# Linear attention feeding two MLP stages: constant matmuls at the start, key and query projections issued together, the first half's routing moved to later groups

## The chip, the cores and the metric

One Trainium2 chip, one core of it. The metric is device time in microseconds (us) of one launch, the median of several runs. A profiled execution of the same kernel gives the rows; its times count from the start of its span. The engines are named as the profile names them: PE (TensorE matmul), PEld (its weight loads), DVE (VectorE), ACT (ScalarE), POOL (GpSimd) and SP (SyncE, which issues most DMAs).

## The reference, cut to what matters

```python
# q, k, v: (4, 8, 576, 64); w_phi: (64, 128)
def phi(x):
    proj = einsum('bhsd,df->bhsf', x, w_phi)
    proj = proj - max(abs(proj), axis=-1, keepdims=True)
    return concatenate([exp(proj), exp(-proj)], axis=-1)
q_p, k_p = phi(q), phi(k)
kv = einsum('bhsf,bhsd->bhfd', k_p, v); z = sum(k_p, axis=2)
x = einsum('bhsf,bhfd->bhsd', q_p, kv) / (einsum('bhsf,bhf->bhs', q_p, z) + 1e-6)
# x as 2304 rows of 512: each row goes to the expert (of 8) with the largest
# cosine similarity: x = gate * (relu(x @ w1[e]) @ w2[e])
# then a dense MLP: h = x @ w_in; out = max(0.01 * h, h) @ w_out
```

## The kernel before, in words

Three stages follow each other on the core: attention with routing folded into it (to about 240 us), the expert MLP, and the dense MLP. Every engine runs its instructions in the order in which the program issues them; nothing reorders them. So the order of the Python statements is the order of each queue.

**Attention** (`attention`, line 63) works in 8 units of a batch pair and a head pair, 9 chunks of 128 rows each: 72 chunks, two to a group, so 36 groups and a loop of 38 steps (line 312). Step t issues in this order:

- `proj(t, "k")` (line 145): six PE matmuls of 256 columns into one of three banks `pj`, then on DVE an absolute maximum (L158) and a subtraction (L160) of 128x512.
- `k_exp` of the group before on ACT (L165, L166), loads of the next unit, and `split_in`, which splits raw keys and queries into a high part (ACT, L101) and a low part (POOL; DVE for the very first).
- `kv_fin_c` (line 215) for a unit whose keys are all in: small PE matmuls (L220) and two DVE copies into `kvz` (L224).
- `kv_mm` of group t-2 (L184, 16 PE matmuls). After a unit's last chunk `kv_fin_a` copies its sums on ACT (L201, L203); when that chunk is the first of its group, the group's other half (`rest`) comes later in the step, since it writes the same banks.
- `proj(t, "q")`: the same six matmuls and two DVE instructions for the queries.
- `q_T` of group t-1: four PE transposes into the only bank `dt` (L190), two exponentials on ACT (L193, L194).
- `flush` (squares on ACT, stores of attention rows by SP), the `rest`, `kv_fin_b` (L211 and an ACT copy `kvt`, L213).
- `num(t-8)` (line 227): 16 PE matmuls that read `kvz` (L243), and on DVE a reciprocal and a scaling (L257 to L262). The first `num` of a unit comes in the same step as that unit's `kv_fin_c`. `num`, `kv_fin_b`, `kv_fin_c` and the fillers share two banks `nm`.
- `filler(t)` (line 1406): work of the later stages. With e = t - 26, e from 0 to 9, it holds the routing of the first 1152 rows: one-hot and counts (e = 0, 1), `choose` and `early_rows` (e = 2), `early_rows2`, `early_place` (e = 3), `is_first`, `first_place` (e = 4), three thirds of `marks_v` (L666; e = 3, 4, 5), `early_ids` with nine small PE matmuls that read all marks (L581) and two gathers by POOL (e = 5), four weight loads (e = 6), `e_x`, which transposes the gathered rows and splits them on ACT and DVE (L931, L952, L953; e = 7), and `moe.split` of weight chunks 0 to 3 (ACT L906, DVE L907; two at e = 8, two at e = 9, with loads of chunks 4 to 7).

After step 37 the last six `num` run (lines 371 to 376), each after a call of `tail`, which splits weight chunks 4 and 5 on the way. `setup_en1` to `setup_en3` prepare the expert embeddings in steps 2 to 4.

Of the kernel before, what the change touches and what calls it, by code (L numbers as in the profile page):

```python
# [8 lines left out]
F32 = mybir.dt.float32  # L9
# [16 lines left out]
F64_MIN = 2.0  # L26
F64_MAX = 2.0 ** 16 * (122880.0 - 2.0 ** -7)
LAG = 8
SPL = {3: (0, "k"), 4: (0, "q"), 6: (1, "k"), 7: (1, "q")}
KL = 2  # L30
QL = 1
# [31 lines left out]
def attention(ctx, late_ctx, tc, consts, in_p, kqT, vx, w_phi, emb, tau, xd, lg, nsq, filler, tail, stores):  # L63
    nc = tc.nc
# [6 lines left out]
    ps_nm, kv_ctx = psum("ps_nm", 2), late_ctx.enter_context(ExitStack())  # L71
# [9 lines left out]
    def load(u, js=(0, 1)):  # L81
        bp, hp = units[u]
        d = st[u]
        for j in js:
            s, e = CUT[j]
            d["raw", j] = in_p.tile([128, 2, 640], F32, tag="raw", name="raw")
            for i in (slice(0, 1), slice(1, 2)) if u == 0 else (slice(0, 2),):
                nc.sync.dma_start(out=d["raw", j][:, i, 0:e - s], in_=kqT[bp, hp, :, i, s:e])
# [6 lines left out]
    def split_in(u, j, nms=("k", "q"), eng=None):  # L95
        d = st[u]
        for nm in nms:
            n = CUT[j][1] - CUT[j][0]
            d[nm, j] = in_p.tile([128, 2, 640], F32R, tag=nm, name=nm)
            raw, hi, lo = d["raw", j][:, "kq".index(nm), 0:n], d[nm, j][:, 0, 0:n], d[nm, j][:, 1, 0:n]  # L100
            nc.scalar.activation(hi, raw, AF.Copy)  # L101
            (eng or nc.gpsimd).tensor_tensor(lo, raw, hi.bitcast(F32), ALU.subtract)

    def setup():
        wb = cp.tile([128, 256], F32, name="wb")
        nc.scalar.dma_start(out=wb, in_=w_phi)
        whi = cp.tile([128, 256], F32R, name="whi")
        wlo = cp.tile([128, 256], F32R, name="wlo")
        nc.vector.tensor_copy(whi, wb)
        nc.vector.tensor_tensor(wlo, wb, whi.bitcast(F32), ALU.subtract)  # L110
        consts["w"] = (whi, wlo)
        nc.vector.memset(cp.tile([128, 16], F32, name="cpad"), 0.0)
# [32 lines left out]
    def proj(t, nm):  # L145
        whi, wlo = consts["w"]
        p = ps_pj.tile([128, 512], F32, tag="pj", name="pj")
        for i, (u, c) in enumerate(groups[t]):
            j = int(c >= 4)
            hi, lo = st[u][nm, j][:, 0], st[u][nm, j][:, 1]  # L150
            s = slice((c - 4 * j) * 128, (c - 4 * j) * 128 + 128)
            o = p[:, i * 256:(i + 1) * 256]
            nc.tensor.matmul(o, hi[:, s], whi, start=True, stop=False)
            nc.tensor.matmul(o, hi[:, s], wlo, start=False, stop=False)
            nc.tensor.matmul(o, lo[:, s], whi, start=False, stop=True)
        pv = p.rearrange("p (g f) -> p g f", f=128)
        m = sm.tile([128, 4, 1], F32, tag="m" + nm, name="m")
        nc.vector.tensor_reduce(m[:, :, 0], pv, X, ALU.max, apply_absolute_value=True)  # L158
        dd = wk.tile([128, 4, 128], F32, tag="d" + nm, name="dd")
        nc.vector.tensor_tensor(dd, pv, m.to_broadcast([128, 4, 128]), ALU.subtract)  # L160
        return dd

    def k_exp(dd):
        kp = wk.tile([128, 2, 4, 128], F32, tag="kp", name="kp")
        nc.scalar.activation(kp[:, 0], dd, AF.Exp)  # L165
        nc.scalar.activation(kp[:, 1], dd, AF.Exp, scale=-1.0)  # L166
        return kp
# [127 lines left out]
    wk = Pools(tc, ctx, "a_wk", {"dk": 3, "dq": 2, "kp": KL + 1})  # L295
    ps_pj, ps_dt = [ctx.enter_context(tc.tile_pool(name=n, bufs=b, space=PSUM, side="right")) for n, b in (("ps_pj", 3), ("ps_dt", 1))]
    load(0)
    setup()
    split_in(0, 0, eng=nc.vector)
    load_v(0)  # L300
# [11 lines left out]
    for t in range(T + 2):  # L312
        more = t < T
        if more:
            dk = proj(t, "k")
        if t - 1 in dks:
            kps[t - 1] = k_exp(dks.pop(t - 1))
        if more:
            dks[t] = dk
            for u, c in groups[t]:  # L320
                if c == 0 and u < U - 1:
                    load(u + 1, (0,) if u == 0 else (0, 1))
                if c == 2 and u == 0:
                    load(1, (1,))
                if c == 6 and 0 < u < U - 1:
                    load_v(u + 1)
                if c in SPL and u + 1 < U:
                    split_in(u + 1, *SPL[c])
        while post:
            kv_fin_c(post.pop())  # L330
        due = [i for i in sorted(kps) if i <= t - KL or not more]
        rest, last = [], fin
        fin = []
        for i in due:
            kp = kps.pop(i)
            g = groups[i]
            kv_mm(i, 0, kp)
            if g[0][1] == 8:
                kv_fin_a(g[0][0])
                fin.append(g[0][0])  # L340
                rest.append((i, kp))
            else:
                kv_mm(i, 1, kp)
                if g[1][1] == 8:
                    kv_fin_a(g[1][0])
                    fin.append(g[1][0])
        if more:
            dq = proj(t, "q")
        for i in sorted(dqs):
            if i <= t - QL and t < T or t > T or i < T - 1 and t == T:  # L350
                qps[i] = q_T(dqs.pop(i))
        if more:
            dqs[t] = dq
        flush()
        for i, kp in rest:
            kv_mm(i, 1, kp)
        if not more:
            last, fin = last + fin, []
        for u0 in last:
            kv_fin_b(u0)  # L360
            post.append(u0)
        if ready() and (done <= t - LAG or not more):
            num(done, qps.pop(done))
            done += 1
        if t in (2, 3, 4):
            (setup_en1, setup_en2, setup_en3)[t - 2](*et)
        if more:
            filler(t, ps)
# [1016 lines left out]
def body(ctx, tc, kqT, vx, w_phi, emb, tau, wm, wd, out):  # L1385
    nc = tc.nc
# [6 lines left out]
    consts = {"ident": ident}  # L1393
    xd = dram.tile([NT, DM], F32, name="xd")
    yt = dram.tile([4, 128, YW], F32, name="yt")
    with tc.manual_schedule(), ExitStack() as r_ctx:
        ff = Ffn(tc, yt, wd, out)
        ro = ff.ro = Router(r_ctx, tc, lambda: ff.open_w(r_ctx))
        lg, nsq = ro.lg, ro.nsq
        with ExitStack() as m_ctx:  # L1400
            moe = Moe(tc, consts, ro, xd, yt, wm)
            moe.open_raw(m_ctx)
# [3 lines left out]
            def filler(n, ps):  # L1406
                if n == CONVERT - 4:
                    ff.fetch(0)
                elif 0 <= n - CONVERT < 7:
                    ff.convert(0, n - CONVERT)  # L1410
                e = n - (18 + LAG)
                if e == 0:
                    ro.onehot(0, 9)
                elif e == 1:
                    ro.rk = ps()[:, 0:10 * NE].rearrange("p (b e) -> p b e", e=NE)
                    ro.count(0, 9)
                    ro.ranks()
                elif e == 2:
                    ro.choose()
                    ro.early_rows()  # L1420
                elif e == 3:
                    ro.early_rows2()
                    ro.early_place()
                elif e == 4:
                    ro.is_first(0, 9)
                    ro.first_place(0, 9)
                if 3 <= e <= 5:
                    ro.marks_v(3 * e - 9, 3 * e - 6)
                if e == 5:
                    ro.early_ids(ps())  # L1430
                    for i in range(NEARLY):
                        moe.gather(i)
                elif e == 6:
                    for c in range(4):
                        moe.load(0, c)
                elif e == 7:
                    moe.e_open()
                    for i in range(NEARLY):
                        moe.e_x(i, ps())
                elif e in (8, 9):  # L1440
                    for c in (2 * e - 16, 2 * e - 15):
                        moe.split(0, c, more=False)
                    for c in (4, 5) if e == 9 else ():
                        moe.load(0, c)
                    for c in (6, 7) if e == 9 else ():
                        moe.load(0, c)

            left = []
# [1 line left out]
            def tail(i):  # L1450

                if not left:
                    left.append(0)
                    ro.ps, ro.ps_k = [r_ctx.enter_context(tc.tile_pool(name=n, bufs=1, space=PSUM, side="right", reuse_waits="tile"))
                                      for n in ("ps_r", "ps_k")]
                    moe.open(m_ctx)
                    ro.rk = ro.ps_k.tile([128, 19, NE], F32, tag="rk", name="rk")
                elif i in (-5, -3):
                    moe.split(0, 4 + (i + 5) // 2, more=False)

# [48 lines left out]
            more = []  # L1509
# [92 lines left out]
```

## Time and profile before

| | before |
|---|---|
| median of 3 runs (lowest, highest) | 910.33 us (909.57, 913.11) |
| the profiled execution's own time | 910.88 us |
| its span in the profile | 909.2 us |
| busy PE / DVE / ACT / POOL | 879.3 / 537.9 / 414.7 / 154.1 us |

The span lies 1.7 us below the time of its own execution. Busy shares are means over stages with different limits, so what counts is which engine ended the waits of PE in the stage that the change touches. The granted clock is the share of TensorE's full speed that was granted in a stretch. A row of the time line gives start, duration, engine, line, the tile written and the tiles read; brackets give the idle time before it and what ended that.

### The profile page before, as it was taken

To read this page: it belongs to the slowest core of one execution; us is meant where nothing else is said; L and a number is where in the kernel's file an instruction comes from. 1 tells how busy PE (TensorE), PEld (TensorE's weight loads), DVE (VectorE), ACT (ScalarE), POOL (GpSimd) and SP (SyncE) were. 2 spreads that over 40 slices of the span, in tenths; PEclk is the share of its full clock that TensorE was granted. 3 is DMA by queue.
4 is the path that set the end of the run, shared out by engine and by line. 5 is a ranking of instruction groups with operands and counts; after the bars stand their busy time and mean duration, and the time that the engine had idled before them with its cause. 6 is when DMAs were issued, how large, how long until landed. Compare 5 with 4: busy or idle time off the path is not lost. (4 is left out here: it accounts for less than half of the span.)

```text
span 909.2 us, 16064 instructions
## 1 busy us (share of the span) xinstructions
PE 879.3 (97%) x6388; PEld 830.8 (91%) x6388; DVE 537.9 (59%) x980; ACT 414.7 (46%) x782; POOL 154.1 (17%) x188
## 2 busy tenths in 40 slices
PE   7999999899999999999999999999999999999996
PEld 6999999899999999999988899999999999999995
DVE  6677666856866236556654576666666666643332
ACT  6777665546335233445555553334333344532221
POOL 4344232211110100101000021111121111101112
PEclk9999999989999999999999999999999999999998
DMA  5442332133166224575742612111111211001111
GB/s 193 158 129 77 106 102 80 49 133 124 52 243 221 79 70 138 193 228 181 231 143 87 194 50 91 47 47 47 48 60 48 79 47 47 1 12 48 47 47 58
DMA packets 40755, 91.66 MB, mean 101 GB/s; under 512 B 3720, under 2 KB 22792, under 8 KB 38624
## 3 DMA queue, kind: packets, MB, share of 16 engines
q1 hardware_dynamic: 37360, 80.13, 26.9%
q0 software_dynamic: 3168, 10.29, 3.4%
q8 instruction: 52, 0.85, 0.4%
q14 instruction: 31, 0.25, 0.1%
q10 hardware_dynamic: 144, 0.13, 0.1%
HBM read 75.53 MB, written 15.01 MB: 100 GB/s over the span
## 5 line engine op out<-in xcount | busy, mean ns | idle before, releaser
L1299 PE MATMUL pl<-xhi,wihi 128*128 128x256 f32 x560 | 157.4, 281 | 1.4 <-PEq L1162 1.4
L1299 PE MATMUL pl<-xlo,wihi 128*128 128x256 f32 x560 | 157.3, 281 | 0.0
L1299 PE MATMUL pl<-xhi,wilo 128*128 128x256 f32 x560 | 157.2, 281 | 0.0
L1304 ACT ACTIVATE t<-pl 128x512 f32<-128x512 f32 x70 | 41.8, 597 | 192.4 <-PE pl L1299 192.4
L1325 PE MATMUL po<-wohi,ghi 128*128 128x512 f32 x288 | 113.8, 395 | 1.3 <-ACT acc L1330 1.3
L1325 PE MATMUL po<-wohi,glo 128*128 128x512 f32 x288 | 114.1, 396 | 0.0
L1325 PE MATMUL po<-wolo,ghi 128*128 128x512 f32 x288 | 113.9, 396 | 0.0
L1113 PE MATMUL py<-hphi,w 128*128 128x256 f32 (+3 forms) x512 | 108.7, 299 | 1.8 <-DVE w L907 1.8
L1299 PEld LDWEIGHTS pl<-xhi,wihi 128*128 128x128 f32 x560 | 106.0, 189 | 4.3 <-issue 1.6
L1305 DVE TENSOR_TENSOR t<-t,pl 128x512 f32<-128x512 f32 x70 | 48.1, 687 | 103.1 <-ACT t L1304 103.1
L1299 PEld LDWEIGHTS pl<-xlo,wihi 128*128 128x128 f32 x560 | 105.4, 188 | 2.8 <-DVE xlo L1283 0.2
L1299 PEld LDWEIGHTS pl<-xhi,wilo 128*128 128x128 f32 x560 | 105.5, 188 | 0.0
L1096 PE MATMUL pp<-phi,w 128*128 128x256 f32 (+3 forms) x512 | 103.7, 296 | 1.5 <-DVE hplo L1099 1.0
L1247 POOL TENSOR_TENSOR af<-af,wraw 128x512 int32<-128x512 int32 x32 | 47.7, 1510 | 310.1 <-DVE af L1245 310.0
L907 DVE TENSOR_TENSOR w<-raw,w 128x1024 fp32r<-128x1024 f32 x64 | 76.9, 1223 | 16.2 <-ACT w L906 16.2
L1113 PEld LDWEIGHTS py<-hphi,w 128*128 128x128 f32 x512 | 83.8, 188 | 2.6 <-DVE w L907 2.4
L1096 PEld LDWEIGHTS pp<-phi,w 128*128 128x128 f32 x512 | 82.9, 189 | 1.9 <-DVE hplo L1099 1.3
L1096 PE MATMUL pp<-plo,w 128*128 128x256 f32 (+3 forms) x256 | 75.8, 296 | 0.0
L1113 PE MATMUL py<-hplo,w 128*128 128x256 f32 (+3 forms) x256 | 75.6, 295 | 0.0
L184 PE MATMUL kv<-v,kp 128*128 128x65 f32 (+1 forms) x576 | 72.4, 279 | 3.2 <-ACT kp L165 1.5
L184 PEld LDWEIGHTS kv<-v,kp 128*128 128x128 f32 x576 | 69.9, 197 | 4.3 <-ACT kp L165 2.0
L243 PE MATMUL nm<-kvz,qp 128*128 128x73 f32 (+1 forms) x576 | 71.2, 279 | 2.2 <-DVE kvz L224 1.6
(320 smaller groups left out, 1718.9 us busy)
## 6 DMA issues: line engine op xcount, KB each, us to landing
raw<-in_wm_dram SPq DMA_DIRECT2D x64, 512.0 KB, 4.5
wraw<-in_wd_dram SPq DMA_DIRECT2D x16, 1024.0 KB, 4.9
v<-in_v_dram SPq DMA_DIRECT2D x8, 650.0 KB, 4.3
raw<-in_kq_dram SPq DMA_DIRECT2D x7, 640.0 KB, 4.7
xd<-xs SPq DMA_DIRECT2D x32, 128.0 KB, 1.8
raw<-in_kq_dram SPq DMA_DIRECT2D x7, 512.0 KB, 4.2
y<-yt SPq DMA_DIRECT2D x6, 512.0 KB, 4.6
yt<-y SPq DMA_DIRECT2D x16, 128.0 KB, 5.0
```

Of the source, the lines that this page charges most:

```text
L184: nc.tensor.matmul(o, kp[:, f, 2 * i + h, :], r, start=(c == 0 and f == 0), stop=(c == 8 and f == 1), skip_group_check=True)
L243: nc.tensor.matmul(ov, qp[:, f, 2 * i + h, :], r, start=(f == 0), stop=(f == 1))
L907: (eng or nc.vector).tensor_tensor(lo, raw, hi.bitcast(F32), ALU.subtract)
L1096: nc.tensor.matmul(pv[:, m], a[:, c], x[:, k], start=(k == 0 and i == 0), stop=(k == 3 and i == 2))
L1113: nc.tensor.matmul(p, a[:, c], b[:, k], start=(k == 0 and n == 0), stop=(k == 7 and n == 2))
L1247: nc.gpsimd.tensor_tensor(f[:, h], f[:, h], d["li"][:, h], ALU.add)
L1299: nc.tensor.matmul(pv[:, m], a[:, c], x[:, k], start=(k == 0 and n == 0), stop=(k == 3 and n == 2))
L1304: nc.scalar.activation(t, p, AF.Copy, scale=0.01)
L1305: nc.vector.tensor_tensor(t, t, p, ALU.max)
L1325: nc.tensor.matmul(p, a[:, cc], x[:, w], start=(b == bs[0] and k == 0 and n == 0), stop=(b == bs[-1] and k == 1 and n == 2))
```

## The change

It issues 30 matmuls of a constant 128x128 bf16 tile of ones ahead of everything else on PE; their result is not read. It issues the query projection of a step right behind the key projection, so ahead of `k_exp`, `kv_fin_c` and `kv_mm`. It moves routing in `filler`: `early_place` from e = 3 to 4, the thirds of `marks_v` from 3, 4, 5 to 4, 5, 6, `is_first` and `first_place` from 4 to 8, `early_ids` and the gathers from 5 to 7, `e_open` and `e_x` from 7 to 9; chunk 0 is split at e = 8, chunks 1 and 2 at e = 9, chunk 3 in the first call of `tail`.

```diff
+WARM = 30
...
+    def warm():
+        p = ps_nm.tile([128, 512], F32, tag="nm", name="nw")
+        for i in range(WARM):
+            nc.tensor.matmul(p[:, 0:128], consts["ones"], consts["ones"], start=True, stop=True)
...
     load(0)
+    warm()
     setup()
...
         if more:
-            dk = proj(t, "k")
+            dk, dq = proj(t, "k"), proj(t, "q")
...
-        if more:
-            dq = proj(t, "q")
         for i in sorted(dqs):
...
+        consts["ones"] = ro.ones
...
                     ro.early_rows2()
+                elif e == 4:
                     ro.early_place()
-                elif e == 4:
+                elif e == 8:
                     ro.is_first(0, 9)
                     ro.first_place(0, 9)
-                if 3 <= e <= 5:
-                    ro.marks_v(3 * e - 9, 3 * e - 6)
-                if e == 5:
+                if 4 <= e <= 6:
+                    ro.marks_v(3 * e - 12, 3 * e - 9)
+                if e == 7:
                     ro.early_ids(ps())
                     for i in range(NEARLY):
                         moe.gather(i)
                 elif e == 6:
                     for c in range(4):
                         moe.load(0, c)
-                elif e == 7:
+                elif e == 8:
+                    moe.split(0, 0, more=False)
+                elif e == 9:
                     moe.e_open()
                     for i in range(NEARLY):
                         moe.e_x(i, ps())
-                elif e in (8, 9):
-                    for c in (2 * e - 16, 2 * e - 15):
+                    for c in (1, 2):
                         moe.split(0, c, more=False)
-                    for c in (4, 5) if e == 9 else ():
-                        moe.load(0, c)
-                    for c in (6, 7) if e == 9 else ():
+                    for c in range(4, 8):
                         moe.load(0, c)
...
                     ro.rk = ro.ps_k.tile([128, 19, NE], F32, tag="rk", name="rk")
+                    moe.split(0, 3, more=False)
                 elif i in (-5, -3):
```

## Rows read from the trace of the kernel before

**Rows 1.** The page: busy time, and the granted clock in 40 slices.
```profile
PE 879.3 (97%) x6388; PEld 830.8 (91%) x6388; DVE 537.9 (59%) x980; ACT 414.7 (46%) x782; POOL 154.1 (17%) x188
...
PEclk9999999989999999999999999999999999999998
```

**Rows 2.** Windows: busy us of each engine, granted clock, DMA share, GB/s.
```profile
172.00:176.00 4.00, 3.87 (x23) 3.87 (x24) 3.70 (x12) 3.24 (x9) 3.59 (x5) 0.67 0.11 33
176.00:180.00 4.00, 4.00 (x34) 4.00 (x34) 3.38 (x7) 1.39 (x5) 0.00 (x0) 0.91 0.02 4
180.00:184.00 4.00, 2.65 (x29) 2.56 (x29) 2.62 (x8) 1.42 (x4) 1.80 (x3) 0.95 0.24 46
184.00:188.00 4.00, 4.00 (x21) 4.00 (x20) 1.56 (x3) 0.39 (x1) 0.95 (x1) 0.50 0.96 346
188.00:192.00 4.00, 4.00 (x26) 4.00 (x26) 1.11 (x7) 2.42 (x8) 0.00 (x0) 0.70 0.74 296
```

**Rows 3.** Time line of PE around two waits: step 30, and the matmuls of `early_ids`.
```profile
172.13 1.11 PE L243 MATMUL nm<-kvz,qp 128*128 128x73 f32 x8 [1.18 <-DVE kvz L224]
...
181.76 0.23 PE L581 MATMUL ex<-qe,r 128*128 128x6 bf16 x3 [1.35 <-DVE r L666]
```

**Rows 4.** Time line of PE in the start, first `num` included.
```profile
4.66 0.58 PE L153 MATMUL pj<-whi,k 128*128 128x256 f32 x1 [4.66 <-ACT k L101]
...
9.57 0.28 PE L153 MATMUL pj<-whi,q 128*128 128x256 f32 x1
...
20.30 2.30 PE L184 MATMUL kv<-v,kp 128*128 128x130 f32 x16 [1.54 <-ACT kp L165]
...
41.97 1.90 PE L243 MATMUL nm<-kvz,qp 128*128 128x73 f32 x16
...
47.42 1.90 PE L243 MATMUL nm<-kvz,qp 128*128 128x73 f32 x16
```

**Rows 5.** Time line of ACT in the start.
```profile
12.08 0.63 ACT L101 ACTIVATE k<-raw 128x512 fp32r<-128x512 f32 x1 [2.81 <-DMA raw<-in_kq_dram]
...
20.15 0.61 ACT L166 ACTIVATE kp<-dd 128x512 f32<-128x512 f32 x1
```

**Rows 6.** Waits of PE from 0 to 145 us: total, times, longest.
```profile
PE kv L184 <- ACT kvz L203: 1.4, 2, 0.8
PE ke L220 <- ACT kvt L213: 0.5, 1, 0.5
```

**Rows 7.** Time line of PE, a query projection of step 28.
```profile
156.41 0.36 PE L153 MATMUL pj<-whi,q 128*128 128x256 f32 x1
156.61 0.28 PE L154 MATMUL pj<-wlo,q 128*128 128x256 f32 x1
156.73 0.28 PE L155 MATMUL pj<-whi,q 128*128 128x256 f32 x1
```

**Rows 8.** Time line of DVE, end of step 29 to step 31.
```profile
169.73 0.17 DVE L572 TENSOR_TENSOR qe<-iota,s 128x18 bf16<-128x18 f32 x1
...
170.50 0.68 DVE L158 TENSOR_REDUCE m<-pj 128x4 f32<-128x512 f32 x1
...
171.90 0.28 DVE L224 COPY kvz<-ke 128x32 f32<-128x32 f32 x2
...
174.25 0.88 DVE L547 TENSOR_TENSOR sc<-oh,oe 128x72 f32<-128x72 bf16 x1
...
176.20 0.55 DVE L666 TENSOR_TENSOR r<-io,rwf 128x384 bf16<-128x384 f32 x1
```

**Rows 9.** Time line of DVE, PE, ACT and PE, steps 34 to the last `num`.
```profile
204.94 2.38 DVE L907 TENSOR_TENSOR w<-raw,w 128x1024 fp32r<-128x1024 f32 x2 [0.16 <-ACT w L906]
...
208.80 2.01 PE L243 MATMUL nm<-kvz,qp 128*128 128x73 f32 x16 [0.41 <-DVE kvz L224]
...
212.03 0.61 ACT L165 ACTIVATE kp<-dd 128x512 f32<-128x512 f32 x1
...
230.99 1.98 PE L243 MATMUL nm<-kvz,qp 128*128 128x73 f32 x16 [0.47 <-DVE xs L262]
```

## The prediction

> **What bounds the kernel now.** The page comes first: PE is busy for 97% of the span, and its granted clock is at nine tenths or more in every slice but two, the last and the ninth, about 182 to 205 us [rows 1]. So a gain has to come from PE's waits or from its clock, and the ninth slice lies where the first half is routed. Windows of 4 us, laid around that slice, show the clock at 0.67, 0.91, 0.95, 0.50 and 0.70 [rows 2]. PE's time line shows what came before each fall: a wait of 1.18 us in step 30 for the `kvz` copy on DVE, and one of 1.35 us for the marks that `early_ids` reads [rows 3]. [...] In the start, PE idles until 4.66 us and again 1.54 us at 20.30 us, for the key exponentials on ACT [rows 4], and less for `kvz` and `kvt` [rows 6]. From the first `num` at 41.97 us a step lasts 5.45 us (the next `num` starts at 47.42) [rows 4], and up to step 29 PE waits once, for `kvz`, 0.6 us (the 1.4 us less the 0.8 of the start) [rows 6]. The later stages are bound by PE, so what attention gains or loses reaches the end whole.
>
> **The change part by part.** Times go against the profiled execution's own 910.88 us, 0.55 us above the median of 910.33.
>
> **Constant matmuls: nothing.** From 4.66 to 9.57 us PE issues 21 matmuls, 0.23 us each; later they follow each other in 0.12 us [rows 4, 7]. A full clock from the first one on would save up to 21 x 0.11 = 2.3 us there. But PE then stands at 20.30 us until ACT has the key exponentials, and ACT's queue runs without a gap from 12.08 us, when a DMA lets it go on, to the second of these at 20.15 us [rows 4, 5]. None of that depends on how early PE was; what PE wins, it waits longer. With that cover gone the value would be the 2.3 us. Thirty matmuls of 128 columns need no more than half the 0.23 us of 256 columns each, about 3.4 us (an estimate), less than the 4.66 us for which PE is idle; were they twice as long, the delay would fall into the same wait. The row says 0. [...]
>
> **Order of the projections, start: -1.2 us.** In step 4 the query projection, 6 x 0.12 = 0.7 us, now lies in front of the wait that ends at 20.30 us and fills it. In step 8 it lies in front of L220, whose 0.5 us wait for `kvt` it covers [rows 6]. Bounds: 0, if `dt`, the single bank for the transposes, holds PE instead, and 2.0 us, if the first wait for `kvz` (0.8 us) goes too. I take 0.7 + 0.5, since both waits are certain to be preceded by work now.
>
> **Order, steps 9 to 29: -1.7 us.** The first matmul of a projection keeps the second waiting for 0.20 us, others 0.12 [rows 7]. Two projections back to back have one such start fewer per step: 21 steps x 0.08 us. Bounds: 0, if the start of `q_T` behind `kv_mm` costs as much, and 1.7 us. Inside a group no such pause shows when a second chunk follows, so I take 1.7.
>
> **Routing, removed: -1.35 and -5.1 us.** All marks are made by e = 6 and `early_ids` comes at the end of e = 7, a full step later, so its wait goes. If no other wait takes its place, the clock's 5.1 us go as well. The gathers, two steps later, still have two steps until `e_x`; POOL's additions behind them are read only after attention. SP's loads of chunks 4 to 7 keep their place but wait for a later split, and the stores of attention rows queue behind them; the four `xs` buffers cover that.
>
> **Routing and order, step 30: +0.6 us.** DVE is behind in step 30: it runs gapless into the `kvz` copy at 171.90 us. What is taken from in front of it is 169.73 to 170.50 us, 0.77 us. What the new order puts there is the query pair, as long as the key pair, 170.50 to 171.90, 1.40 us [rows 8]. The wait of 1.18 us becomes 1.8.
>
> **Step 35: +1.7 us.** The same copy for the next unit kept PE for 0.41 us behind two weight splits, 2.38 us on DVE [rows 9]. Now one split of 1.19 stands there and `is_first` with `first_place`, 174.25 to 176.20 us, 1.95 [rows 8]: 0.76 us more, and the query pair, 1.40. Bounds +1.4 (the extra falls into time in which the splits wait for ACT anyway) and +2.2. The wait becomes 1.8 to 2.6 us.
>
> **Steps 35 and 36: +0.9 us.** The key exponentials of group 35, at 212.03 us behind two splits [rows 9], now also stand behind two evacuations of `e_x` of 0.6 us, which wait for transposes that follow the delayed `num`. Bounds 0.3 and 1.5 us; I take the middle. `e_x` itself only moves.
>
> **Tail: +1.2 us.** The split of chunk 3, half of 2.38 us, enters DVE's queue ahead of the last six `num`, where PE already waits for DVE's `xs` [rows 9]. Bounds 0.7 (0.47 us of slack) and 1.2.
>
> **Sum.** -1.2 - 1.7 - 1.35 - 5.1 + 0.6 + 1.7 + 0.9 + 1.2 = -4.95: 905.9 us if the clock never falls. But the walk leaves waits of about 1.8 us in step 30, over 2 in step 35, over 1 in step 36. In the attention stage three waits exceeded 1 us: 1.54 (clock stayed full), 1.18 and 1.35 (it fell). I take one fall at the price of the shorter stretch, 1.7 us: **907.6 us**.
>
> **Rivals.**
> - The clock holds: 905.9 us. For it: after 1.54 us at 20.30 the clock stayed full. Against: shorter waits brought it down twice. [...]
> - The start pays: ACT's chain moves with PE after all, 907.6 - 2.3 = 905.3 us. Against: the DMA at 12.08 us.
> - DVE isn't late: nothing is left of the waits in steps 30, 35 and 36, so from 905.9 go 1.8, 2.1 and 0.9: 901.1 us. For: DVE is busy 59% over all. Against: step 30 already waits for DVE with less in front.
> - Two falls: 905.9 + 2 x 1.7 = 909.3 us.
> - Slower, through the new order on DVE: the `kvz` copy stands behind the query pair, PE waits in steps 30, 35 and 36, and after each the clock stays low for the longer stretch, 3.4 us: 905.9 + 10.2 = 916.1 us. It decides from three such falls on; with two it is 912.7.
>
> **How the numbers follow.** Chances: forecast 0.34, clock holds 0.16, start pays 0.05, DVE not late 0.14, two falls 0.23, three long falls 0.08. A measurement of this kernel tells about 0.5% (4.6 us) from no change; against 910.33 that is below 905.8 or above 914.9. Faster: DVE not late 0.14, half of the clock holding 0.08, most of the start 0.04, and a part of the forecast, whose terms with bounds sum to about 3 us to either side, 0.05: 0.31. Slower: three long falls, 0.07. Within: 0.62. The range leaves out most of the last rival and the lower half of "DVE isn't late", and holds two long falls nearly: 902.5 to 912.0 us.
>
> **What would show it.** Right: the first `kv_mm` wait of the start still ends near 20.3 us, and is longer before the query projection fills it; the first `num` at 40 to 41.5 us; steps of 5.37 us up to step 29; no wait at L581; a wait of 1.5 us or more for `kvz` in step 30 and around 2 in step 35, with the granted clock below 1 behind at least one. Wrong: the first `num` before 40 us (the start pays), no `kvz` wait above 1 us (DVE is not late), or a full clock through 160 to 240 us.

## The result, and the profile after

The changed kernel takes 922.52 us (median of 15 executions, 919.95 to 924.14); the kernel before took 910.38 us on the same chips (median of 15, 907.03 to 921.02). The ratio is 1.012, with a 95% interval of 1.0095 to 1.0145: slower by 1.2%, where 907.6 had been forecast. Ratios and intervals, here and below, leave out executions in a slower state, while the times are medians of all, so a ratio differs a little from the quotient of two medians. Single executions of the kernel before spread over 14 us, and those beside the experiments have mean granted clocks from 0.979 (923 us) to 0.998 (906 us): some of them have a clock fall that others lack, so a profile of it is one draw among several.

The profiled execution of the changed kernel has a span of 922.3 us, 13.1 more than before. The page, against [rows 1]:

```profile
PE 890.1 (97%) x6418; PEld 840.5 (91%) x6418; DVE 538.3 (58%) x980; ACT 414.7 (45%) x782; POOL 152.9 (17%) x188
...
PEclk9999999895999999999999899999999999999998
```

PE does 30 matmuls more and is busy 10.8 us longer. Of these, 3.4 us are the constant matmuls, in time in which PE stood idle before, so some 7 of the 13.1 us are slower work and the rest is longer waits. The clock shows where the work is slower: an eight stands in the eighth slice, about 161 to 184 us, a five in the tenth, about 207 to 230 us, and an eight near 510 us. Windows of 6 us of the same kernel (time, PE, PEld, DVE, ACT and POOL busy, clock, DMA share, GB/s):

```profile
168.00:174.00 6.00, 2.32 (x20) 2.18 (x18) 5.28 (x11) 1.77 (x6) 2.12 (x2) 0.88 0.04 13
174.00:180.00 6.00, 6.00 (x33) 6.00 (x32) 4.13 (x10) 1.35 (x3) 0.96 (x3) 0.55 0.08 25
204.00:210.00 6.00, 4.17 (x24) 3.56 (x23) 2.70 (x8) 2.02 (x7) 0.09 (x1) 0.72 0.26 87
210.00:216.00 6.00, 6.00 (x29) 5.98 (x29) 3.75 (x4) 3.88 (x6) 0.34 (x2) 0.50 0.19 53
216.00:222.00 6.00, 5.48 (x27) 5.29 (x26) 0.00 (x0) 2.16 (x9) 0.00 (x0) 0.50 0.64 234
222.00:228.00 6.00, 6.00 (x32) 6.00 (x32) 1.09 (x5) 2.55 (x7) 0.44 (x2) 0.57 0.07 22
...
510.00:516.00 6.00, 3.46 (x16) 3.46 (x17) 1.38 (x3) 0.63 (x1) 0.00 (x0) 0.54 0.46 144
```

What a window loses is put at (1 - clock) x 6 us, an estimate from these clocks. Behind the last of these falls PE's pace goes with it: from 514 to 516 us, at a clock of 0.50, its matmuls of 256 columns start 0.21 us apart, and 0.12 us apart from 500.2 to 502.8 us of the kernel before, at 1.00. By that estimate 3.4 us are lost from 168 to 180, 10.3 us from 204 to 228, where the kernel before had a clock of 1.00 (one of its windows below), and 2.8 us from 510 to 516. The same for the 4 us windows of [rows 2] gives 1.7 us for the first two and 3.4 for the other three: the 5.1 us that the kernel before lost from 172 to 192 are replaced by the 3.4 from 168 to 180.

```profile
210.00:216.00 6.00, 5.28 (x44) 4.87 (x43) 3.25 (x6) 4.49 (x13) 2.21 (x2) 1.00 0.69 240
```

PE's time line in the changed kernel shows what stands ahead of each stretch, and the start:

```profile
1.26 3.38 PE L108 MATMUL nw<-ones 128*128 128x128 bf16 x30 [1.26 <-DVE ones L473]
4.83 0.58 PE L159 MATMUL pj<-whi,k 128*128 128x256 f32 x1 [0.19 <-ACT k L102]
...
20.27 2.30 PE L190 MATMUL kv<-v,kp 128*128 128x130 f32 x16 [0.87 <-ACT kp L171]
...
41.03 1.90 PE L249 MATMUL nm<-kvz,qp 128*128 128x73 f32 x16
...
173.41 1.99 PE L249 MATMUL nm<-kvz,qp 128*128 128x73 f32 x8 [3.68 <-DVE kvz L230]
...
205.89 2.98 PE L249 MATMUL nm<-kvz,qp 128*128 128x73 f32 x16 [1.62 <-DVE kvz L230]
...
508.76 0.35 PE L1304 MATMUL pl<-xhi,wihi 128*128 128x256 f32 x1 [1.47 <-PEq L1167]
512.54 0.58 PE L1304 MATMUL pl<-xlo,wihi 128*128 128x256 f32 x1 [3.42 <-DVE f_pad L1200]
```

The first `pl` matmul of the kernel before:

```profile
499.99 0.35 PE L1299 MATMUL pl<-xhi,wihi 128*128 128x256 f32 x1 [1.40 <-PEq L1162]
```

- **Start.** The constant matmuls end before the first projection, which comes 0.17 us later than before. They do make the projections faster (0.12 us apart from 5.78 us on, where the kernel before, 0.21 us apart from 5.77, gets there at 9.57; the granted clock reads 1.00 in every window from 4 to 10 us of both), but `kv`'s wait takes that back: it still ends at 20.27 us (20.30 in [rows 4]). The first `num` is at 41.03, 0.94 us earlier.
- **Step 30.** The `kvz` wait is 3.68 us, against 1.18 in [rows 3]. The wait of `early_ids` is gone.
- **Step 35.** The `kvz` wait is 1.62 us, against 0.41 in [rows 9]. Behind it the clock is low for some 20 us.
- **Dense stage.** Behind the branch (L1167) a wait of 1.47 us comes ahead of the first `pl` matmul, as before (1.40). A second one, of 3.42 us, stands between the first and the second `pl` matmul; the kernel before has none there. `pl` starts 8.8 us later than before (499.99 there), so 4.3 of the 13.1 us are lost behind that point.

Why step 30 waited three times as long stands on DVE and POOL (time lines of the changed kernel, DVE first):

```profile
167.06 0.16 DVE L599 CAST pos<-ri 128x9 f32<-128x9 int32 x1
167.26 1.39 DVE L600 TENSOR_SCALAR ri<-ri 128x9 int32<-128x9 int32 x1
168.56 0.16 DVE L601 CAST rwf<-rw 128x9 f32<-128x9 int32 x1
168.69 1.46 DVE L602 CAST s<-ri 128x9 f32<-128x9 int32 x1
...
173.18 0.28 DVE L230 COPY kvz<-ke 128x32 f32<-128x32 f32 x2
```
```profile
167.08 1.54 POOL L103 TENSOR_TENSOR k<-raw,k 128x640 fp32r<-128x640 f32 x1
168.58 1.54 POOL L103 TENSOR_TENSOR q<-raw,q 128x640 fp32r<-128x640 f32 x1
```

Two steps of the routing (`rows`), on 9 elements per partition, take 1.39 and 1.46 us. Each ends within 0.03 us of the end of a low-part split on POOL (167.08 + 1.54 = 168.62; 168.58 + 1.54 = 170.12). In the kernel before they took 0.17 and 0.18 us, since POOL's splits began only after them (DVE, ACT and POOL):

```profile
169.04 0.17 DVE L595 TENSOR_SCALAR ri<-ri 128x9 int32<-128x9 int32 x1
...
169.25 0.18 DVE L597 CAST s<-ri 128x9 f32<-128x9 int32 x1
```
```profile
169.94 0.31 ACT L574 ACTIVATE qe<-qe,pidx 128x18 bf16<-128x18 bf16 x1 [4.29 <-DVE qe L572]
```
```profile
171.99 1.55 POOL L102 TENSOR_TENSOR k<-raw,k 128x640 fp32r<-128x640 f32 x1 [3.08 <-ACT k L101]
```

There `early_place`'s step on ACT (L574) waited 4.29 us for DVE, and ACT's high-part splits, which POOL needs, stood behind it. The change moved `early_place` to the next group, so ACT and POOL came early and met the routing. Why the two last until the splits end, no run shows; L599 and L601, which overlap a split too, took 0.16 us.

### The profile page after: what moved, and what is told of

It reads as the page before. It is cut to its first block, busy times and chain, and to the rows that moved or that the text cites. A ratio compares the mean times of both kernels' runs of the same rounds, so it can differ in the third digit from the quotient of the medians.

```text
span 922.3 us, 16137 instructions
## 1 busy us (share of the span) xinstructions
PE 890.1 (97%) x6418; PEld 840.5 (91%) x6418; DVE 538.3 (58%) x980; ACT 414.7 (45%) x782; POOL 152.9 (17%) x188
## 5 line engine op out<-in xcount | busy, mean ns | idle before, releaser
L249 PE MATMUL nm<-kvz,qp 128*128 128x73 f32 (+1 forms) x576 | 74.5, 285 | 6.6 <-DVE kvz L230 5.3
L249 PEld LDWEIGHTS nm<-kvz,qp 128*128 128x128 f32 x576 | 72.3, 202 | 7.4 <-DVE kvz L230 5.7
```

Of the source, the lines that this page charges most:

```text
L249: nc.tensor.matmul(ov, qp[:, f, 2 * i + h, :], r, start=(f == 0), stop=(f == 1))
```

## The experiments

**One part each.** Four kernels take the change apart. Theory: the loss is a `kvz` copy too late on DVE (order), a collision (routing) and a second wait behind the branch (constant matmuls). Rival: one part brings it all, or the parts do nothing alone. The kernel before beside them: 910.02 us.

`warm_only`, the kernel before with the constant matmuls alone:

```diff
     load(0)
+    warm()
     setup()
```


> The kernel before with the 30 constant matmuls alone. Theory A (the longer PE instruction stream shifts what PE has at hand behind the branch ahead of the dense MLP): the start gains nothing, the first num stays at 41.9 to 42.0 us, but a second wait of about 3.4 us shows on PE right behind that branch, followed by a low clock: 4 us or so slower, 914 to 915 us. Rival B (that wait came from the changed times of attention): no such wait, 910 to 911 us.

Measured: 913.92 us, ratio 1.0037 (1.0011 to 1.0062). PE's waits behind the branch (no other `pl` matmul there waits):

```profile
503.20 0.36 PE L1306 MATMUL pl<-xhi,wihi 128*128 128x256 f32 x1 [1.29 <-PEq L1169]
...
506.74 0.37 PE L1306 MATMUL pl<-xlo,wihi 128*128 128x256 f32 x1 [2.48 <-issue]
```

The matmuls alone bring the second wait, 500 us after they ran; here it comes after seven `pl` matmuls. The start gives nothing for them: `kv` still waits 1.5 us. In this profile the clock is also near 0.50 behind that wait, from 22 to 32 us (its mean over the execution is 0.986, against 0.991 in the kernel before), and the first `num` comes 4.4 us later than in the kernel before. There the same wait of 1.54 us left the clock full.

`order_only`, the kernel before with the query projection behind the key projection:

```diff
-            dk = proj(t, "k")
+            dk, dq = proj(t, "k"), proj(t, "q")
...
-        if more:
-            dq = proj(t, "q")
```


> The kernel before with the query projection issued behind the key projection, nothing else. Theory A (the kvz copy behind the query pair on DVE makes PE wait, and the clock that falls in step 35 comes back late because no projections follow): first num about 0.9 us earlier, a kvz wait of 2.3 to 2.8 us in step 30 and of 1.5 to 1.9 us in step 35, the clock at half for 15 us or more behind the latter: 915 to 919 us, no extra wait behind the branch. Rival B (the order is harmless, the routing's new places do the harm): 907 to 909 us.

Measured: 919.73 us, ratio 1.0104 (1.0074 to 1.0134): the largest loss of the three parts. Step 30 waits 1.94 us for `kvz`, where 2.3 to 2.8 had been expected, and the clock stays at 1.00 behind it (first window below); the first `num` is 0.25 us earlier, not 0.9. Step 35, that window, and those behind step 35:

```profile
210.12 2.01 PE L243 MATMUL nm<-kvz,qp 128*128 128x73 f32 x16 [1.72 <-DVE kvz L224]
```
```profile
174.00:180.00 6.00, 4.97 (x50) 4.88 (x49) 5.56 (x16) 2.97 (x9) 0.68 (x4) 1.00 0.08 25
...
210.00:216.00 6.00, 5.88 (x36) 5.88 (x37) 3.25 (x7) 3.17 (x6) 2.21 (x2) 0.67 0.70 249
216.00:222.00 6.00, 5.48 (x27) 5.29 (x26) 0.00 (x0) 2.17 (x9) 0.00 (x0) 0.50 0.01 3
222.00:228.00 6.00, 6.00 (x29) 6.00 (x29) 1.09 (x5) 1.56 (x5) 0.44 (x2) 0.50 0.07 22
```

`route_only`, the change with neither the constant matmuls nor the new order; the routing of groups 3 to 9 is all that is left. Against the change:

```diff
-    warm()
...
-            dk, dq = proj(t, "k"), proj(t, "q")
+            dk = proj(t, "k")
...
+        if more:
+            dq = proj(t, "q")
         for i in sorted(dqs):
```

> The kernel before with the routing moved to its new places, nothing else. Theory A (moving early_place lets ACT and so POOL's low parts run earlier, beside DVE's integer steps of early_rows2): two of these steps take about 1.4 us instead of 0.2 and the kvz wait of step 30 grows to 2.5 to 3 us; no wait for marks; step 35 waits under 1 us and the clock holds there: 908 to 911 us. Rival B (the new places alone make the whole loss): 918 to 922 us.

Measured: 915.46 us, ratio 1.0077 (1.0051 to 1.0104), a miss by 4 to 7 us. The collision is there (the two steps take 1.41 and 1.46 us, step 30 waits 2.94 us for `kvz`). What had not been expected is a fall later on. The `kvz` wait of step 35 is only 0.30 us, but `kv` of group 35 waits for its key exponentials:

```profile
205.44 2.01 PE L249 MATMUL nm<-kvz,qp 128*128 128x73 f32 x16 [0.30 <-DVE kvz L230]
...
212.23 2.29 PE L190 MATMUL kv<-v,kp 128*128 128x65 f32 x16 [1.36 <-ACT kp L171]
```
```profile
210.00:216.00 6.00, 4.03 (x29) 3.62 (x29) 2.86 (x3) 4.28 (x12) 0.00 (x0) 0.87 0.44 139
216.00:222.00 6.00, 6.00 (x30) 6.00 (x30) 1.09 (x5) 0.58 (x1) 0.44 (x2) 0.50 0.48 170
```

`no_warm`, the change without the constant matmuls:

```diff
     load(0)
-    warm()
     setup()
```

> The changed kernel without the constant matmuls. Theory A (they cost about 4.4 us behind the branch ahead of the dense MLP and win nothing at the start): 917 to 919 us, no wait of 3.4 us there. Rival B (that wait belongs to the changed times): 921 to 923 us.

Measured: 919.14 us (five executions, 915.65 to 919.5), ratio 1.0101 (1.0063 to 1.0138), no second wait behind the branch. Against the change that is 3.4 us less.

**One suspect each.** The first four suggest three places; the next kernels mend one each in the change. The kernel before beside them: 910.07 us.

`finc_between`:

```diff
-            dk, dq = proj(t, "k"), proj(t, "q")
+            dk = proj(t, "k")
+            while post:
+                kv_fin_c(post.pop())
+            dq = proj(t, "q")
```


> The changed kernel with one thing moved: the little matmuls on kvt and their copy into kvz (kv_fin_c) stand between key and query projection, where the kernel before has them, so the kvz copy no longer has the query pair's 1.40 us on DVE in front of it. Theory A (the query pair ahead of the kvz copy makes the waits of steps 30 and 35, and these let the clock fall): the kvz wait of step 30 goes from 3.68 to 2.2 to 2.4 us (the split collision of 2.5 us stays), that of step 35 from 1.62 to 0.2 to 0.4; the clock stays at 1.00 from 204 to 228 or falls later for the key-exponentials wait of 1.4 us; the wait of 3.4 us behind the branch stays; time 912 to 917. Theory B (the clock of the last steps falls because of the removed pauses and the light work there, whatever the wait): the kvz waits shrink but 204 to 228 stays at 0.50, time 920 to 923.

Measured: 924.43 us (four executions, 919.38 to 925.85), ratio 1.0108 (1.0036 to 1.018): no gain. Step 30 still waits 3.03 us, where 2.2 to 2.4 had been expected. The `kvz` wait of step 35 is gone (0.29), so that part of theory A holds; but the key-exponentials wait came in its place, 1.36 us at 209.35, with the clock at 0.56, 0.50, 0.50 and 0.50 from 210 to 234 and at 0.66 up to 240. In the change PE was slow there and met the exponentials when they were ready. One wait had hidden the other.

`place3`:

```diff
                     ro.early_rows2()
-                elif e == 4:
                     ro.early_place()
```


> The changed kernel with early_place back in group 3, where the kernel before has it. Theory A (with early_place a group later, ACT does the next unit's splits at once, and POOL's low-part splits run beside two integer steps of early_rows2, which then take 1.4 us each in place of 0.17): L600 and L602 are back near 0.2 us, POOL's splits start some 4 us later, the kvz wait of step 30 is 1.8 to 2.1 us, and the stretch from 164 to 180 is 1.5 to 2.5 us shorter. Step 35, its wait of 1.6 us and the low clock behind it, and the wait behind the branch stay: 919 to 921.5. Theory B (the two steps are slow for a reason of their own, their rows being written by the step before): L600 and L602 stay at 1.4 us, and the time stays at 922.

Measured: 919.58 us, ratio 1.0093 (1.0067 to 1.0118). DVE and POOL:

```profile
166.93 0.17 DVE L600 TENSOR_SCALAR ri<-ri 128x9 int32<-128x9 int32 x1
...
167.14 0.17 DVE L602 CAST s<-ri 128x9 f32<-128x9 int32 x1
```
```profile
169.88 1.54 POOL L103 TENSOR_TENSOR k<-raw,k 128x640 fp32r<-128x640 f32 x1 [3.09 <-ACT k L102]
```

Theory A: the two steps are short again, and POOL starts 2.8 us later. Step 30 waits 1.47 us for `kvz`, under the 1.8 to 2.1 expected, and the clock stays at 1.00 up to 204 us; step 35 waits 1.61 us, and behind it the clock falls.

`fill35`:

```diff
-WARM = 30
+DUM = {27: 28}
+WARM = 2
...
+            for _ in range(DUM.get(t, 0) if i == 0 else 0):
+                nc.tensor.matmul(p[:, 0:128], consts["ones"], consts["ones"], start=True, stop=True)
```


> The changed kernel with 28 of the 30 constant matmuls moved from the start into step 35, into the accumulator of num(27) ahead of its own first matmul, where TensorE sits idle for 1.6 us for the kvz copy; the number of TensorE's instructions stays. Theory A (the idle stretch of 1.6 us is what drops the clock, which then stays low as long as only small matmuls come): the fill covers the wait, the clock stays at 1.00 from 204 to some 214 at least, and 4 to 10 us of the 10 us lost there come back, 912 to 918. Theory B (the clock drops for the light work after step 35, not for the wait): the clock falls all the same between 204 and 228, within 1.5 us of 922.5. For the wait behind the branch: if it hangs on the number of TensorE's instructions ahead of it, it stays at 3.4 us; if it hangs on the constant matmuls at the start, it goes.

Measured: 922.96 us (four executions), ratio 1.0105 (1.004 to 1.0169): no gain, a miss. The fill works, and the clock is 1.00 from 204 to 210:

```profile
203.92 1.73 PE L242 MATMUL nm<-ones 128*128 128x128 bf16 x28
205.70 2.01 PE L252 MATMUL nm<-kvz,qp 128*128 128x73 f32 x16
...
212.49 0.44 PE L191 MATMUL kv<-v,kp 128*128 128x65 f32 x2 [1.36 <-ACT kp L172]
```

but the key-exponentials wait shows up again, and the clock is at 0.75, 0.50 and 0.61 from 210 to 228. The wait behind the branch stays at 3.45 us with only two constant matmuls left at the start and 28 in step 35: it does not hang on where they stand.

`combo`: the edits of `finc_between` and `place3` together, without the constant matmuls. Against the change:

```diff
-    warm()
...
-            dk, dq = proj(t, "k"), proj(t, "q")
+            dk = proj(t, "k")
+            while post:
+                kv_fin_c(post.pop())
+            dq = proj(t, "q")
...
                     ro.early_rows2()
-                elif e == 4:
                     ro.early_place()
```

> The changed kernel with three things undone: no constant matmuls, kv_fin_c between the two projections, early_place in group 3. What is left of the change is the query projection behind the key projection in all other steps and the rest of the routing's moves. Theory A (the loss is the sum of a wait behind the branch, a kvz copy that came too late in steps 30 and 35, and the collision of splits with routing, each with its low clock): the kvz wait of step 30 is under 0.8 us, that of step 35 under 0.4, no second wait behind the branch, the clock at 1.00 through 162 to 204; 904 to 911, level with or under the kernel before (910.4); if the key-exponentials wait of 1.4 us near 214 still drops the clock, 910 to 914. Theory B (the removed pauses and the moved routing bring the clock falls by themselves): 914 to 919.

Measured: 912.39 us (908.87 to 918.62), ratio 1.0019 (0.9982 to 1.0055). Steps 30 and 35 wait 0.8 and 0.29 us for `kvz`; the only fall left from 162 to 240 is the one behind `kp`. ACT shows why `kp` is late:

```profile
203.00 1.99 ACT L913 ACTIVATE w<-raw 128x1024 fp32r<-128x1024 f32 x2
204.89 0.62 ACT L171 ACTIVATE kp<-dd 128x512 f32<-128x512 f32 x1
```

**The last wait.** `early_exp`, on top of `combo`:

```diff
         flush()
+        if t == T - 1:
+            kps[t] = k_exp(dks.pop(t))
         for i, kp in rest:
```


> The kernel of combo with one step more: in the last group (35) the key exponentials are issued on ACT within their own step, ahead of that group's routing work, instead of behind it in step 36. In combo ACT gave them at 204.89 to 206.0, behind two copies of gathered rows and two splits of 1024 columns, and kv(35) waited 1.36 us at 205.57, after which the clock was 0.63, 0.50 and 0.74 from 204 to 222. Theory A (that wait alone drops the clock there): no wait for kp, the clock at 1.00 from 198 to 234, some 7 us of span less than combo's 909.4, time 901 to 906 and a ratio to the kernel before under 0.997. Theory B (the clock falls there because after the last projections only small matmuls come, with or without a wait): the clock still falls between 204 and 222, time 908 to 913.

Measured: 903.42 us (11 executions, 902.65 to 904.99) against 910.86 for the kernel before: ratio 0.9909 (0.9878 to 0.9939). ACT and PE, and two windows:

```profile
200.10 0.61 ACT L171 ACTIVATE kp<-dd 128x512 f32<-128x512 f32 x1
...
202.86 1.99 ACT L915 ACTIVATE w<-raw 128x1024 fp32r<-128x1024 f32 x2
```
```profile
202.17 3.68 PE L190 MATMUL kv<-v,kp 128*128 128x65 f32 x32
```
```profile
204.00:210.00 6.00, 5.48 (x50) 5.34 (x50) 3.31 (x7) 2.97 (x10) 0.19 (x1) 1.00 0.60 191
210.00:216.00 6.00, 5.83 (x50) 5.60 (x50) 3.60 (x13) 4.52 (x13) 1.60 (x4) 1.00 0.41 139
```

`kv`'s 32 matmuls run without a break and at full clock. Over the span the clock is 0.998, and the 14 us of spread are 2.3. Apart from the constant ones, the matmuls of the change are all there, in the same steps, so theory B (the clock falls because of what runs in these steps) is out.

`order_finc`: the kernel before, with the projections as in `finc_between`:

```diff
             dk = proj(t, "k")
+            while post:
+                kv_fin_c(post.pop())
+            dq = proj(t, "q")
...
-        if more:
-            dq = proj(t, "q")
```

> The kernel before with the query projection behind the key projection, and kv_fin_c between the two, so that the kvz copy stands on DVE where it stood; no constant matmuls, routing as before. Theory A (of the order's loss of 9 us, 919.73, all comes from the kvz copy behind the query pair): kvz waits of steps 30 and 35 under 0.6 us, the clock at 1.00 from 204 to 234, the fall behind the 1.35 us wait of early_ids stays; time 905 to 911. Theory B (the clock falls in the last steps because the projections no longer stand between the small matmuls): low clock between 204 and 234, time 914 to 920.

Measured: 908.63 us, ratio 0.9979 (0.9939 to 1.0019), 11 us under `order_only`: the order's loss was the `kvz` copy behind the query pair. Its ten executions fall into two groups, six from 905.71 to 909.89 us and four from 914.86 to 916.17. The profiled one is of the latter (span 914.4): it still has a low clock from 216 to 228, behind a wait of only 0.52 us.

**The wait behind the branch.** The kernel before with other numbers of constant matmuls, one execution each. `warm15` and `warm60`, against `warm_only`:

```diff
-WARM = 30
+WARM = 15
```


> The kernel before with 15 constant matmuls at the start in place of 30. Theory A (the matmuls move the later instructions in TensorE's stream, and whether a second wait stands behind the branch ahead of the dense stage, and after which matmul, hangs on their number): the wait of 2.5 us after the first pl matmul is gone or stands at another matmul; first pl wait 1.2 to 2 us. Theory B (the matmuls at the start bring it through data or timing): the wait stays after the first pl matmul with 2 to 3.5 us. kv's wait at the start and its end at 20.3 us unchanged in both.

```diff
-WARM = 30
+WARM = 60
```


> The kernel before with 60 constant matmuls at the start in place of 30: they end near 7 us, still ahead of the key exponentials at 20.15, so the start stays where it is (kv's wait ends at 20.3). Theory A (place in TensorE's stream): the second wait behind the branch is gone or stands at another matmul than with 30. Theory B (the matmuls themselves): it stays after the first pl matmul, 2 to 3.5 us.

With 15 (911.2 us) the second wait is 0.81 us, after 22 `pl` matmuls instead of the seven of `warm_only`:

```profile
503.55 0.28 PE L1306 MATMUL pl<-xlo,wihi 128*128 128x256 f32 x1 [0.81 <-issue]
```

With 60 there is none. That execution (919.95 us) has a low clock from 216 to 240 behind a wait of 0.52 us; its time and mean clock (0.982) are those of the slower executions of the kernel before. So the second wait changes with the number of constant matmuls: 15 more bring it 15 `pl` matmuls earlier (22 to 7). In all seven kernels that have it, PE goes on 3.4 to 3.9 us after its first `pl` matmul, however many came in between. What PE waits for there, no run shows.

**Prices in a kernel whose clock holds.** The terms of the sum could not be read off kernels that carry a fall, so one thing each was changed in `early_exp` (903.42 us). `held_warm`:

```diff
     load(0)
+    warm()
     setup()
```


> The kernel of early_exp, whose clock holds (0.998), with the 30 constant matmuls put back at the start. Theory A (they buy nothing at the start, and cost a second wait behind the branch): kv's wait at the start ends within 0.3 us of where it ended, a wait of 2.5 to 3.5 us stands after the first pl matmul, and the time is 903.4 plus 2.5 to 4.5 = 906 to 908. Theory B (they win 0.5 us or more at the start where the clock holds afterwards, and the loss belonged to the disturbed kernel): under 903.

`held_old_order`:

```diff
             dk = proj(t, "k")
-            while post:
-                kv_fin_c(post.pop())
-            dq = proj(t, "q")
...
+        if more:
+            dq = proj(t, "q")
```


> The kernel of early_exp with the query projection back at the end of the step. Theory A (the order is worth what the spans of the steps showed, 0.94 us at the start and 0.9 us over steps 9 to 29, once no late copy takes it back): 903.4 plus 1.5 to 2.5 = 905 to 906. Theory B (the order is worth nothing, the gain of early_exp being all routing): 903 to 904. Theory C (the order is needed for the clock to hold): over 908.

`held_place4`:

```diff
                     ro.early_rows2()
+                elif e == 4:
                     ro.early_place()
```


> The kernel of early_exp with early_place in group 4, as the change has it. Theory A (that move alone lets POOL's splits run beside the integer steps of group 3): L600 and L602's counterparts take 1.4 us each, the kvz wait of step 30 goes from 0.81 to 2.3 to 3.3 us, and the time is 903.4 plus 1.7 to 2.5, or plus 4 to 6 if the clock falls behind it: 905 to 909. Theory B (the wait is covered there): 903 to 904.

Measured: 907.46, 905.07 and 907.65 us, with ratios to the kernel before (912.12 us beside them) of 0.9962 (0.9944 to 0.998), 0.9935 (0.9903 to 0.9966) and 0.9948 (0.9918 to 0.9979): all three times by theory A, though the second wait of `held_warm` stands after the fourth `pl` matmul, not the first. So, by medians of two launches on one chip, the constant matmuls cost 4.0 us, the order gains 1.7, and `early_place` in group 4 costs 4.2; the key exponentials behind the splits (`combo`, on another chip) cost about 9.0. The 1.7 is the least certain: in the profile of `held_old_order` the clock is at 0.72 from 20 to 26 us, and PE's matmuls of 256 columns start 0.21 us apart from 23.4 to 24.3 us (0.12 in the kernel before, from 22.6 to 23.1), behind `kv`'s wait of 1.54 us, which is 0.18 in `early_exp`. The second wait behind the branch in `held_warm`, the clock behind it, and the collision's wait for `kvz` in step 30 of `held_place4`:

```profile
495.57 0.58 PE L1309 MATMUL pl<-xlo,wihi 128*128 128x256 f32 x1 [2.69 <-issue]
```
```profile
496.00:502.00 6.00, 6.00 (x26) 5.61 (x26) 1.76 (x3) 1.58 (x3) 0.00 (x0) 0.55 0.87 270
```
```profile
172.67 1.98 PE L249 MATMUL nm<-kvz,qp 128*128 128x73 f32 x8 [3.00 <-DVE kvz L230]
```

## Why the prediction was wrong

The prediction named the right places and the right mechanism for the loss, and underpriced what follows a wait. By its own steps:

- **Sum, "one fall at the price of the shorter stretch, 1.7 us": the step that failed.** Two falls came, of 3.4 us (step 30) and 10.3 us (step 35): 12.0 of the 16.4 us by which the profiled execution (923.99 us) missed. Both prices, 1.7 and 3.4 us, came from falls in steps 30 and 31. No run shows them as times, nor their sum of 5.1: they are the author's estimates from the clocks of [rows 2], and what the runs showed in their place are falls of 3.4 and 10.3 us by the same estimate in the change, and none from 162 to 240 us in `early_exp`. Nothing in the rows gave a price for a fall in steps 35 to 37, and the longest stretch seen was taken as an upper end. The "slower" rival had the mechanism, the `kvz` copy behind the query pair, but at 3.4 us per fall it needed three of them; one of 10.3 us cost as much. `order_only` shows it (8.6 us from 210 to 234), `order_finc` takes it back.
- **Constant matmuls, "nothing": right for the start, wrong as a total.** `kv`'s wait ended at 20.27 us. The cost lay where the working did not look, behind the branch: +4.3 us in the profile, +4.0 in `held_warm`. The working had weighed 0 against a gain of 2.3 us, and a cost was not among them.
- **Step 30, +0.6 us.** The wait became 3.68 us, not 1.8. The working took early steps out of DVE's queue and left the rest at their durations; it did not follow ACT's queue, where the moved step had been holding back the splits. `place3` undoes 2.2 us of it. Without the routing's moves the query pair brought the wait from 1.18 to 1.94 (`order_only`), about half of the 1.40 us counted.
- **Routing removed, -1.35 and -5.1 us.** The `early_ids` wait went, as said, and the fall from 181 to 192 with it; 3.4 us came back in step 30.
- **Step 35, +1.7 us.** The wait was 1.62, below the 1.8 to 2.6 given, and 0.3 us (`route_only`) without the query pair: the order made it, and `is_first` and the splits did not.
- **Steps 35 and 36, +0.9 us.** The wait for the key exponentials is 1.36 us where it shows (`route_only`, `combo`), inside the bounds of 0.3 and 1.5. In the change it is covered by the slow clock. As a cause of a fall it costs about 9.0 us.
- **Tail, +1.2 us.** The waits of the last six `num` for `xs` are 0.42 and 0.71 us, against 0.47 in [rows 9]: +0.7, the lower bound.
- **Order, start -1.2 and steps 9 to 29 -1.7.** Measured -0.94 at the first `num`, and -1.83 in all at step 30 (163.48 against 165.31 us for its first projection), so -0.9 for the steps, about half of what was counted. The -0.9 is the same, within 0.03 us, in all eleven kernels with the new order. The start is less sure: their first `num` comes at 41.03 us in the change, at 41.44 in `early_exp`, 41.63 in `held_place4` and 41.90 in `held_warm`. The order may also hold the clock in the start: it shortens `kv`'s wait there to 0.18 to 0.89 us, and none of these eleven profiles has a fall behind it; of the six with the old order two have one (5.2 and 1.7 us).
- **"The clock holds" (0.16).** The waits of 1.36 to 1.72 us in `route_only` and `order_only`, each with a clock near 0.50 behind it, speak against it. But the rows that the prediction set against this rival were draws too: behind step 30's wait of 1.2 us the clock fell in the kernel before and `warm15` and stayed full in `warm_only` and `warm60`, and behind the 1.54 us of the start it stayed full in the kernel before and `warm15` and fell in `warm_only` and `held_old_order`.

The parts don't add up to the loss one by one. On `early_exp` they sum to 4.0 + 4.2 + 9.0 = 17.2 us, and the change is 19.1 us above it. The late `kvz` copy and the late exponentials stand ahead of the same stretch, so mending either alone gave nothing (`finc_between`, `fill35`), and mending both gave all of it.

Open: why a clock falls behind 0.52 us in one execution (`order_finc`, `warm60`) and holds behind 1.47 (`place3`) or 1.94 (`order_only`, step 30) in another. The length of one wait does not decide it in these runs. Removing the waits above 1 us in steps 30 to 36 left a mean clock of 0.996 to 0.998 in all 11 executions of `early_exp`, but the kernel before has executions of both kinds with the same program.

## What to carry to other kernels

Price a new wait by the clock stretch behind it, and take that from the stage where the wait would lie; where no row shows one, a fall there belongs into the range at more than the longest seen. Whether the clock falls behind a wait takes several executions to tell: one profile is one draw. When a wait is mended and nothing comes of it, look for the next wait ahead of the same stretch before dropping the theory: here two had to go together. And when a step is moved, follow what it held back on its queue as well as what it waited for: the early splits on POOL cost 4.2 us (`held_place4`), where what had been moved took 0.77 us of DVE [rows 8].

## What was not expected of the hardware

- **A second wait behind a branch that comes and goes with the number of constant matmuls.** 0 of them: no second wait. 15: 0.81 us, after 22 `pl` matmuls. 30: 2.5 to 3.5 us, in every kernel with 30, wherever they stand (`fill35`), after the first, the fourth or the seventh. 60: none. It ends 3.4 to 3.9 us after the first `pl` matmul wherever it comes.
- **The clock's fall is dear late in attention.** Falls behind waits of 1.36 to 1.72 us in steps 35 and 36 cost from 5.2 us (`route_only`) to 13.7 us (`finc_between`), by (1 - clock) x 6 us per window; those up to step 31 cost 1.7 to 5.2 us.
- **9-element steps on DVE that take as long as a 640-column split on POOL** (1.39 and 1.46 against 0.17 us), and only two of the six in a row, those that start 0.18 and 0.11 us after the start of a split. L601 between them, at 168.56 us, starts 0.06 us before the end of one and takes 0.16.
